# Decoding weights beside attention: one PSUM bank per unit's exponents, another order of the units, and one step earlier in a slot

## The chip, the cores and the metric

The kernel runs on one core of a Trainium2 chip. The metric is the device time of one execution in microseconds (us): 1356.4 us before the change, the median of three runs (1355.92 to 1356.41).

In the names of the profile, PE is the matrix engine (PEld its weight loads), DVE the vector engine, ACT the scalar (activation) engine, POOL the general-purpose engine, and SP the engine that issues the transfers. Each engine takes its instructions strictly in order, so an instruction that waits holds up everything behind it on its engine.

## The reference

Top-32 attention over 8 batches of 8 heads (sequence 576, head size 64), then a gated feed-forward block over the 4608 tokens:

```
scores = q @ k.T / sqrt(64)                      # per batch and head, 576 x 576
kth    = 32nd largest score of each row
attn   = softmax(where(scores >= kth, scores, -1e9))
x      = (attn @ v), heads side by side          # 4608 x 512
a, b   = x @ w1, x @ w2                          # 4608 x 1024 each
out    = ((a * b) @ w3) @ w_out                  # w3 1024 x 1024, w_out 1024 x 512
```

The weights reach the kernel as 64-bit floating-point numbers, seen as pairs of 32-bit words. Each has to be turned into 32-bit form on the chip ("decoding"). The product w3 @ w_out is formed once on the chip ("folding", tiles `pf`, `wf`), and each weight is split into a high and a low part (`wh` and `wl`, `wf[0]` and `wf[1]`) for the matmuls.

## The kernel before, in words

Attention is cut into 144 **slots**, 18 per batch; a slot is 128 query rows of two heads. Slots are pipelined over four turns p of one loop: turn p computes the scores of slot p+1 (`st`, copied to `s`), finds the 32 largest scores of slot p (DVE), masks and exponentiates slot p-1 (ACT and POOL, `pab`), and transposes slot p-2 (`tp`), multiplies it by v (`ro`) and stores it (`xt`). The feed-forward block of a batch (`ab`, `eo`) starts about two slots after the batch's last attention slot; from then on `fill` hands PE 32 of its matmuls per slot. Every engine's instructions stay in the order in which this Python code issues them.

DVE's part of a turn is a list of steps (`top32_steps`): the reciprocal of the row sums, a fold of four elementwise operations (`w`), three rounds of `MAX8` and `MATCH_REPLACE8`, a last pair of `MAX8` over 576 columns, and the store of `xt`. POOL's masking (`pab<-s,pab`) waits for the fold by an explicit dependency (lines 260 to 265).

The weights are decoded beside the first attention slots, in 80 **units** of 128x256 weights. `warm()` (line 473) is called five times in a turn, lines 497, 513, 516, 533 and 543; they are called places A to E here. Each call moves every running unit on by one step, oldest first, and starts one new unit. So units are started in the first 16 slots. A unit's steps, one for each call (lines 108 to 146):

1. ACT writes the unit's exponents `t` into PSUM and the low bits `y` into SBUF (lines 123 and 124).
2. DVE reads `t` twice, writing `z` (sign) and `y` (lines 127 and 128).
3. POOL adds the two halves of `y`.
4. Nothing.
5. For w3, PE multiplies the unit by the decoded w_out into `pf` (two matmuls; four units make one `pf`); for w1 and w2, ACT copies to `wh`. One call later come ACT's copy `wf<-pf` or POOL's `wl`, and after `wf<-pf`, another call later, DVE's `wf<-pf,wf`.

`t` and `pf` come from the same PSUM pool, `ps_m`, with three banks of 512 numbers per partition. A `t` has 256. Before, two units that follow each other share a bank (lines 106 and 114 to 117): the first takes columns 0 to 255, the second 256 to 511. The layer that sets the semaphores orders accesses by bank, so the second unit's ACT write waits until DVE has finished reading the first unit.

The units stand in a list (lines 396 to 403): 16 of w_out, then sixteen times w3, w1, w3, then 16 of w2.

Of the kernel before, what the change touches and what calls it, by code (L numbers as in the profile page):

```python
# [9 lines left out]
F32 = mybir.dt.float32  # L10
# [12 lines left out]
NCC, NFC, NEC = DM // 128, DF // 128, DM // 128  # L23
# [33 lines left out]
def attn_moe(ctx: ExitStack, tc: tile.TileContext, q, k, v, w1, w2, w3, w_out, out, flag, general):  # L57
# [23 lines left out]
    ps_m = ctx.enter_context(tc.tile_pool(name="ps_m", bufs=3, space=PSUM))  # L81
# [21 lines left out]
        sp.dma_start(z[:, :512].bitcast(I32), src)  # L103
        return z

    bank = []

    def decode(z, dst=None):

        if not bank:
            both = ps_m.tile([128, 512], F32, tag="mm", name="t")
            bank.extend((both[:, 256:], both[:, :256]))
        t = bank.pop()
        y = x_p.tile([128, 2 * HS], F32, tag="x", name="y")
        high = z[:, 1:512:2]
        low = z[:, :512].bitcast(U16)[:, 1:1024:4]  # L120
        u, r = y[:, :256].bitcast(I32), y[:, 256:512].bitcast(I32)
        sign = z[:, :256].bitcast(I32)
        act.activation(t, high, AF.Copy, scale=2.0**-112)
        act.activation(r, low, AF.Copy, scale=2.0**-13)
        yield
        ti = t.bitcast(I32)
        dve.tensor_scalar(sign, ti, -(2**31), None, op0=ALU.bitwise_and)
        dve.scalar_tensor_tensor(u, ti, 3, sign, op0=ALU.logical_shift_left, op1=ALU.bitwise_or)
        yield
        dst = y[:, :256] if dst is None else dst  # L130
        pool.tensor_tensor(dst.bitcast(I32), u, r, op=ALU.add)
        yield
        yield
        return dst

    def load_w12(i, c, z):
        if len(wl) == i:
            wl.append(const.tile([128, NCC * DF], F32R, tag="wl1", name="wl1"))
        cut = slice(c * 256, (c + 1) * 256)
        y = yield from decode(z)  # L140
        act.copy(wh[i][:, cut], y)
        yield
        pool.tensor_tensor(wl[i][:, cut], y, wh[i][:, cut].bitcast(F32), op=ALU.subtract)

    def load_wout(c, z):
        yield from decode(z, wo[:, c * 256 : (c + 1) * 256])
# [3 lines left out]
    def load_w3(c, z):  # L150
        f, i = c // 4, c % 4
        y = yield from decode(z)
        if i == 0:
            fold[f] = ps_m.tile([128, 512], F32, tag="mm", name=f"pf{f}")
        for j in range(2 * i, 2 * i + 2):
            pe.matmul(
                fold[f], y[:, (j % 2) * 128 : (j % 2 + 1) * 128], wo[:, j * DM : (j + 1) * DM],
                start=(j == 0), stop=(j == NFC - 1),
            )
        if i == 3:  # L160
            cut = slice(f * DM, (f + 1) * DM)
            yield
            act.copy(wf[0][:, cut], fold[f])
            yield
            dve.tensor_tensor(wf[1][:, cut], fold[f], wf[0][:, cut].bitcast(F32), op=ALU.subtract)
# [44 lines left out]
    def top32_steps(s, slot):  # L210

        w = att_p.tile([128, 2, S], F32, tag="w", name="w", bufs=1)
        top = tops[slot % len(tops)]
        one, two, three = slice(0, NG), slice(NG, 2 * NG), slice(2 * NG, S)
        dve.tensor_tensor(w[:, :, three], s[:, :, one], s[:, :, two], op=ALU.max)  # L220
        dve.tensor_tensor(w[:, :, two], s[:, :, one], s[:, :, two], op=ALU.min)
        dve.tensor_tensor(w[:, :, one], w[:, :, three], s[:, :, three], op=ALU.max)
        yield dve.tensor_tensor(w[:, :, three], w[:, :, three], s[:, :, three], op=ALU.min)
        for i in range(4):
            cut = slice(i * 8, (i + 1) * 8)
            for a in range(2):
                dve.max(top[:, a, cut], w[:, a, one] if i < 3 else w[:, a, :])
            if i < 3:
                for a in range(2):
                    dve.match_replace(w[:, a, one], top[:, a, cut], w[:, a, one], NEG)  # L230
                yield

    def edges_of(slot):
        top = tops[slot % len(tops)]
        edge = small.tile([128, 2, 2], F32, tag="edge", name="edge")
        pool.tensor_tensor(edge, top[:, :, 0:32:31], coef, op=ALU.mult)
        pool.tensor_tensor(over[:, 2 * slot : 2 * slot + 2], top[:, :, 31], top[:, :, 23], op=ALU.subtract)
        return edge
# [15 lines left out]
    def new_weights():  # L254
        return att_p.tile([128, 2, S], F32, tag="pab", name="pab"), small.tile([128, 2], F32, tag="sums", name="sums")
# [15 lines left out]
    def invert(sums):  # L271
        pool.tensor_scalar(sums, sums, 1e-9, None, op0=ALU.add)
        dve.reciprocal(sums, sums)
# [13 lines left out]
    def take_turned(tp, ro):  # L287
        pts = att_p.tile([128, 2, 512], F32, tag="pts", name="pts", bufs=1)
        act.copy(pts, tp)
        pr = att_p.tile([128, 128], F32, tag="pr", name="pr")  # L290
        act.copy(pr, ro[:, :128])
        return pts, pr
# [101 lines left out]
                yield  # L394

    startup = [(w_out[c], lambda z, c=c: load_wout(c, z)) for c in range(16)]
    for c in range(16):
        startup += [
            (w3[2 * c], lambda z, c=c: load_w3(2 * c, z)),
            (w1[c], lambda z, c=c: load_w12(0, c, z)),  # L400
            (w3[2 * c + 1], lambda z, c=c: load_w3(2 * c + 1, z)),
        ]
    startup += [(w2[c], lambda z, c=c: load_w12(1, c, z)) for c in range(16)]

    def new_xt():
# [52 lines left out]
    def pairs_of(i):  # L458
        return [kv[u] for u in slots[i][0]]

    def fetch_pair(u):
        if u < B * NHP:
            kv[u] = load_pair(u // NHP, u % NHP)
# [4 lines left out]
    def prefetch(n):  # L468
        while waiting and len(fetched) < n:
            src, step = waiting.pop(0)  # L470
            fetched.append((fetch(src), step))

    def warm():

        if p < 0:
            return
        if fetched:
            z, step = fetched.pop(0)
            going.append(step(z))
        going[:] = [unit for unit in going if next(unit, "end") != "end"]  # L480
        prefetch(5)
# [5 lines left out]
    for p in range(-1, n_slots + 3):  # L487
        i, j, m = p + 1, p - 1, p - 2
        if i < n_slots and slots[i][1] == 3:
            fetch_pair(slots[i][0][0] + 2)  # L490
        while starting:
            queue.append(moe_steps(*starting.pop(0), put_off.append))
        finder = top32_steps(ss[p], p) if 0 <= p < n_slots else iter(())
        if 0 <= m < n_slots:
            invert(pabs[m][1])
        folded = next(finder, None)
        warm()
        if 0 <= j < n_slots:
            edges[j] = edges_of(j)
            pabs[j] = new_weights()  # L500
            for a in range(2):
                mask(ss[j], edges[j], pabs[j][0], a, folded if a == 0 else None)
        fill(SHARE[0])
        next(finder, None)
        if 0 <= m < n_slots:
            tp, ro = turn(pabs[m][0])
            pts, pr = take_turned(tp, ro)
        if 0 <= j < n_slots:
            exps(edges[j], *pabs[j], 0)
        if ready and (m + 1) % NS:  # L510
            put_off.append(lambda x=ready[0]: split_x(x[2], x[1], 0, 1))
            starting.append(ready.pop(0))
        warm()
        fill(SHARE[1])
        next(finder, None)
        warm()
        if i < n_slots:
            st = scores(pairs_of(i), slots[i][1])
            ss[i] = new_s()
            take_scores(ss[i], st, 0)  # L520
        if 0 <= j < n_slots:
            exps(edges[j], *pabs[j], 1)
        if i < n_slots:
            take_scores(ss[i], st, 1)
        if 0 <= m < n_slots:
            us, t = slots[m]
            for u in us:
                if u not in xts:
                    xts[u] = new_xt()
            ov, rb = values([kv[u][2] for u in us], t, pts, pr, pabs[m][1], ro)  # L530
            rec = take_rb(rb)
        next(finder, None)
        warm()
        fill(SHARE[2])
        for _ in finder:
            pass
        if 0 <= m < n_slots:
            store_x([xts[u] for u in us], t, ov, rec)
            del ss[m], pabs[m], edges[m]
            if (m + 1) % NS == 0:  # L540
                ready.append((m // NS, [xts[m // NS * NHP + hp] for hp in range(NHP)], ([], [])))
                put_off.append(lambda x=ready[0]: split_x(x[2], x[1], 0, 0))
        warm()
# [63 lines left out]
```

## Time and profile before

| | |
|---|---|
| median of three runs | 1356.4 us |
| the profiled execution | 1356.2 us, of which its span is 1354.3 us |
| PE busy | 1253.2 us, 93% of the span |
| DVE busy | 1156.7 us, 85% |
| ACT busy | 981.6 us, 72% |
| POOL busy | 785.0 us, 58% |

The span is cut into 40 slices of 34 us in the page's overview. PE stands at 9 tenths or more from the ninth slice to the last but one; before that it is between 2 and 8 tenths. In those early slices DVE shows 7 to 9 tenths. The stretch in which weights are decoded is read with its own windows below, since shares over the whole span mix it with the long stretch behind it.

### The profile page before, as it was taken

Reading aid. Unit: us, or ns where it says so; the run is one execution under the profiler, and the core shown is the slowest. Engines: PE = TensorE matmul, PEld = TensorE weight load, DVE = VectorE, ACT = ScalarE, POOL = GpSimd, SP = SyncE. Lnnn points to the kernel's source line nnn. Section 1 sums busy time; section 2 is a strip of 40 time slices with the busy share of each in tenths; the row PEclk is TensorE's granted clock in tenths of the full one; section 3 lists DMA queues with packets and bytes.
Section 4 is the critical chain, followed back from the end, with each engine's and each line's share of the span. In section 5 each row is a group of like instructions: output and inputs, shape, how many; then the busy total and the mean of one; then the engine's idle time right before and its main releaser. Section 6 shows DMA issues by size and latency. Waiting matters only on the chain.

```text
span 1354.3 us, 31309 instructions
## 1 busy us (share of the span) xinstructions
PE 1253.2 (93%) x11153; PEld 1081.8 (80%) x11153; DVE 1156.7 (85%) x4060; ACT 981.6 (72%) x2169; POOL 785.0 (58%) x1033
## 2 busy tenths in 40 slices
PE   2678855899999999999999999999999999999996
PEld 1444433688989999898988898988899888989996
DVE  7998898999999999999989999999899998998100
ACT  4767777777777877787777877777777777777321
POOL 3666677665665656664656565665656565646220
PEclk6799887999999999999999999999999999999998
DMA  6443430102011111001020202010110101000000
GB/s 219 110 130 95 126 108 30 30 13 66 12 48 31 43 35 35 32 17 62 12 67 12 67 12 67 12 48 30 44 36 24 43 17 62 12 19 1 18 19 21
DMA packets 34746, 63.98 MB, mean 47 GB/s; under 512 B 3860, under 2 KB 12052, under 8 KB 34580
## 3 DMA queue, kind: packets, MB, share of 16 engines
q1 hardware_dynamic: 34580, 61.88, 14.6%
q8 instruction: 90, 1.47, 0.5%
q14 instruction: 76, 0.62, 0.1%
HBM read 52.43 MB, written 9.44 MB: 46 GB/s over the span
## 4 chain that ended last, share of the span: by engine, by line
PE 77%; DVE 13%; ACT 5%; issue 2%; POOL 2%; DMA 0%; DVEq 0%; SPq 0%; POOLq 0%; ACTq 0%
PE ab L48 29%; PE eo L48 15%; PE ro L48 14%; PE st L48 10%; PE tp L48 8%; DVE w L48 5%; DVE top L48 4%; ACT pab L48 2%; DVE y L48 2%; DVE z L48 2%; ACT pts L48 1%; ACT y L48 1%; POOL wl L48 1%; ACT t L48 1%; POOL y L48 0%
## 5 line engine op out<-in xcount | busy, mean ns | idle before, releaser
L48 POOL TENSOR_TENSOR pab<-s,pab 128x576 f32<-128x576 f32 x288 | 403.4, 1423 | 242.9 <-DVE w L48 184.7
L48 DVE MAX8 top<-w 128x8 f32<-128x192 f32 (+1 forms) x1152 | 466.7, 446 | 0.0
L48 PE MATMUL ab<-xf,wh 128*128 128x288 f32 x2048 | 432.7, 300 | 0.0
L48 PEld LDWEIGHTS ab<-xf,wh 128*128 128x128 f32 x2048 | 332.9, 188 | 8.5 <-issue 7.5
L48 PE MATMUL ab<-xf,wl 128*128 128x288 f32 x1024 | 309.5, 302 | 0.0
L48 ACT ACTIVATE pab<-s,edge 128x576 f32<-128x576 f32 x288 | 208.0, 771 | 116.2 <-POOL edge L48 115.8
L48 DVE MATCH_REPLACE8 w<-top,w 128x192 f32<-128x192 f32 x864 | 289.1, 342 | 0.0
L48 PE MATMUL st<-kt,qt 64*128 64x288 f32 (+1 forms) x1280 | 191.2, 444 | 61.0 <-ACT pts L48 51.7
L48 ACT ACTIVATE pab<-pab,edge 128x576 f32<-128x576 f32 x288 | 224.9, 781 | 20.9 <-POOL pab L48 20.5
L48 PE MATMUL eo<-g,wf 128*128 128x288 f32 x1536 | 228.2, 300 | 0.0
L48 PEld LDWEIGHTS eo<-g,wf 128*128 128x128 f32 x1536 | 208.3, 188 | 7.0 <-issue 7.0
L48 PEld LDWEIGHTS ab<-xf,wl 128*128 128x128 f32 x1024 | 192.5, 188 | 4.8 <-issue 4.8
L48 ACT COPY pts<-tp 128x1024 f32<-128x1024 f32 x144 | 145.5, 1011 | 61.8 <-PE tp L48 57.4
L48 PEld LDWEIGHTS st<-kt,qt 64*128 64x128 f32 (+1 forms) x1280 | 97.8, 181 | 115.5 <-ACT pts L48 61.6
L48 ACT COPY s<-st 128x576 f32<-128x576 f32 x288 | 181.8, 631 | 9.9 <-PE st L48 9.9
L48 POOL TENSOR_TENSOR g<-whole,g 128x288 fp32r<-128x288 f32 x128 | 103.1, 805 | 113.9 <-ACT g L48 109.9
L48 PE MATMUL tp<-ident,pab 128*128 128x128 f32 x1152 | 152.7, 275 | 16.3 <-ACT s L48 15.4
L48 DVE TENSOR_TENSOR w<-w,s 128x384 f32<-128x384 f32 x288 | 160.0, 555 | 4.9
L48 DVE TENSOR_TENSOR w<-s 128x384 f32<-128x384 f32 x288 | 155.8, 581 | 7.5 <-ACT s L48 7.5
L48 PE MATMUL ro<-pts,vt 128*64 128x128 f32 (+1 forms) x2560 | 161.1, 271 | 0.0
L48 PEld LDWEIGHTS tp<-ident,pab 128*128 128x128 f32 x1152 | 134.4, 142 | 25.5 <-POOL wo L48 13.2
L48 PEld LDWEIGHTS ro<-pts,vt 128*64 128x64 f32 x2560 | 141.3, 143 | 0.0
(49 smaller groups left out, 1275.5 us busy)
## 6 DMA issues: line engine op xcount, KB each, us to landing
z<-in_w SPq DMA_DIRECT2D x64, 256.0 KB, 2.6
vt<-in_v SPq DMA_DIRECT2D x32, 352.0 KB, 3.7
kt<-in_k SPq DMA_DIRECT2D x32, 320.0 KB, 3.5
qt<-in_q SPq DMA_DIRECT2D x32, 288.0 KB, 3.0
out_t<-osb SPq DMA_DIRECT2D x64, 144.0 KB, 1.7
z<-in_wo SPq DMA_DIRECT2D x16, 256.0 KB, 5.2
flag<-missed SPq DMA_DIRECT2D x1, 0.0 KB
seen<-flag SPq DMA_DIRECT2D x1, 0.0 KB
```

Of the source, the lines that this page charges most:

```text
L48: ins = fn(*args, **kw)
```

## The change

`decode` no longer shares a bank: each unit's `t` is a tile of its own, of which it uses half. The units of w3 and w1 stand in another order: four of w3 (one whole `pf`), then two of w1. And the call of `warm()` at place B moves ahead of the slot's first exponential (`exps(..., 0)`).

```
     def decode(z, dst=None):
-        if not bank:
-            both = ps_m.tile([128, 512], F32, tag="mm", name="t")
-            bank.extend((both[:, 256:], both[:, :256]))
-        t = bank.pop()
+        t = ps_m.tile([128, 512], F32, tag="mm", name="t")[:, :256]
...
-    for c in range(16):
-        startup += [
-            (w3[2 * c], lambda z, c=c: load_w3(2 * c, z)),
-            (w1[c], lambda z, c=c: load_w12(0, c, z)),
-            (w3[2 * c + 1], lambda z, c=c: load_w3(2 * c + 1, z)),
-        ]
+    for f in range(NFC):
+        startup += [(w3[c], lambda z, c=c: load_w3(c, z)) for c in range(4 * f, 4 * f + 4)]
+        startup += [(w1[c], lambda z, c=c: load_w12(0, c, z)) for c in range(2 * f, 2 * f + 2)]
...
             pts, pr = take_turned(tp, ro)
+        warm()
         if 0 <= j < n_slots:
             exps(edges[j], *pabs[j], 0)
         if ready and (m + 1) % NS:
             put_off.append(lambda x=ready[0]: split_x(x[2], x[1], 0, 1))
             starting.append(ready.pop(0))
-        warm()
         fill(SHARE[1])
```

What this does to ACT's order shows in the eighth slot, the one whose fold starts at 93.95 us in the trace of before. In before, ACT has there, from the last unit of the slot before (place E) to the unit of place B (`t_907` is one bank, used twice; `pab,sums` is the exponential):

```order
L48 ACTIVATE t_907<-z_770 128x256
...
L48 ACTIVATE t_907<-z_787 128x256
L48 ACTIVATE y_931<-z_787 128x256
L48 ACTIVATE pab_939<-s_725,edge_936 128x576 x2
L48 COPY pts_960<-tp_949 128x1024
L48 COPY pr_962<-ro_958 128x128
L48 ACTIVATE pab_939,sums_940<-pab_939,edge_936 128x576
L48 CAST wh0_98<-y_841 128x256
L48 ACTIVATE t_969<-z_827 128x256
L48 ACTIVATE y_970<-z_827 128x256
```

In the changed kernel the same stretch of ACT's order reads (every `t` has a number of its own):

```order
L48 ACTIVATE t_924<-z_785 128x256
...
L48 ACTIVATE t_948<-z_803 128x256
L48 ACTIVATE y_949<-z_803 128x256
L48 ACTIVATE pab_957<-s_740,edge_954 128x576 x2
L48 COPY pts_978<-tp_967 128x1024
L48 COPY pr_980<-ro_976 128x128
L48 CAST wf0_100<-pf2_851 128x512
L48 CAST wh0_98<-y_858 128x256
L48 ACTIVATE t_987<-z_843 128x256
L48 ACTIVATE y_988<-z_843 128x256
L48 ACTIVATE pab_957,sums_958<-pab_957,edge_954 128x576
```

The unit of place B, with the copies of older units, now stands ahead of the exponential instead of behind it. Through the pool, from the first `pf` to the last every `pf` gets the same bank, and the `t` of successive units alternate between the other two: `t_987` waits for DVE to have read the unit two before it, `t_924`.

On PE, in the same slot, the fold's matmuls stood in before as follows, from the transposes to the end of the values:

```order
L48 MATMUL tp_949<-ident_85,pab_792 128x128 x8
L48 MATMUL ro_958<-ident_85,pab_792 128x128
L48 MATMUL pf2_834<-wo_102,y_892 128x512 x2
L48 MATMUL st_990<-kt_122,qt_120 128x288 x2
...
L48 MATMUL pf3_1019<-wo_102,y_908 128x512 x2
L48 MATMUL pf3_1019<-wo_102,y_970 128x512 x2
```

And in the changed kernel:

```order
L48 MATMUL pf2_851<-wo_102,y_840 128x512 x2
L48 MATMUL tp_967<-ident_85,pab_808 128x128 x8
L48 MATMUL ro_976<-ident_85,pab_808 128x128
L48 MATMUL st_1010<-kt_122,qt_120 128x288 x2
...
L48 MATMUL pf3_1039<-wo_102,y_925 128x512 x2
L48 MATMUL pf3_1039<-wo_102,y_949 128x512 x2
L48 MATMUL pf3_1039<-wo_102,y_988 128x512 x2
```

A `pf` is now filled by units that follow each other, and some calls of `warm()` issue no matmul. The next `pf` starts in the call after DVE's `wf<-pf,wf` of the one before, whose bank it takes over.

## Rows read from the trace of the kernel before

**Rows 1.** The page, busy time, share of the span and instructions of each engine.

```profile
PE 1253.2 (93%) x11153; PEld 1081.8 (80%) x11153; DVE 1156.7 (85%) x4060; ACT 981.6 (72%) x2169; POOL 785.0 (58%) x1033
```

**Rows 2.** Windows: four stretches, and what the columns are.

```profile
core 0: us, PE busy (x) PEld busy (x) DVE busy (x) ACT busy (x) POOL busy (x), PEclk, DMA share, GB/s
20.00:206.00 186.00, 128.33 (x714) 71.60 (x714) 167.92 (x520) 133.59 (x326) 123.50 (x163) 0.84 0.40 116
206.00:256.00 50.00, 31.39 (x267) 22.30 (x268) 45.09 (x159) 38.79 (x86) 35.31 (x47) 0.82 0.09 28
256.00:300.00 44.00, 43.80 (x422) 38.79 (x420) 41.42 (x149) 33.69 (x72) 27.07 (x35) 1.00 0.08 24
300.00:1250.00 950.00, 950.00 (x9009) 853.69 (x9010) 881.10 (x3177) 742.55 (x1608) 571.16 (x747) 1.00 0.11 35
```

**Rows 3.** Waits, 20 to 206: who waited for whom, us, times, longest.

```profile
ACT t L48 <- DVE y L48: 53.1, 34, 4.3
...
DVE z L48 <- ACT y L48: 9.2, 7, 1.8
...
DVE wf L48 <- ACT wf L48: 2.5, 2, 1.2
```

**Rows 4.** Waits of DVE, 206 to 290.

```profile
DVE sums L48 <- POOL sums L48: 3.3, 4, 1.1
DVE z L48 <- ACT y L48: 2.0, 2, 1.8
```

**Rows 5.** Timeline, slot from 93.95: start, us, instruction [idle before, releaser].

```profile
93.54 0.42 DVE L48 SCALAR_TENSOR_TENSOR y<-t,z 128x256 int32<-128x256 int32 x1
...
93.95 1.53 DVE L48 TENSOR_TENSOR w<-s 128x384 f32<-128x384 f32 x2
94.11 0.96 POOL L48 TENSOR_TENSOR y<-y 128x256 int32<-128x256 int32 x1 [0.32 <-DVE sums L48]
...
95.41 1.14 DVE L48 TENSOR_TENSOR w<-w,s 128x384 f32<-128x384 f32 x2
...
96.92 0.42 DVE L48 SCALAR_TENSOR_TENSOR y<-t,z 128x256 int32<-128x256 int32 x1
...
97.38 0.40 ACT L48 ACTIVATE t<-z 128x256 f32<-128x256 f32 x1 [4.07 <-DVE y L48]
...
98.04 1.42 ACT L48 ACTIVATE pab<-s,edge 128x576 f32<-128x576 f32 x2
...
98.87 2.77 POOL L48 TENSOR_TENSOR pab<-s,pab 128x576 f32<-128x576 f32 x2 [2.86 <-DVE z L48]
...
100.42 0.78 ACT L48 ACTIVATE pab<-pab,edge 128x576 f32<-128x576 f32 x1
...
101.48 0.40 ACT L48 ACTIVATE t<-z 128x256 f32<-128x256 f32 x1
...
101.82 0.44 ACT L48 ACTIVATE y<-z 128x256 int32<-128x256 uint16 x1
...
102.28 0.42 DVE L48 TENSOR_SCALAR z<-t 128x256 int32<-128x256 int32 x1 [1.80 <-ACT y L48]
...
106.70 0.68 DVE L48 TENSOR_TENSOR wf<-pf,wf 128x512 fp32r<-128x512 f32 x1
```

**Rows 6.** Timeline, the next slot, to the fold of the one behind it.

```profile
108.24 1.54 DVE L48 TENSOR_TENSOR w<-s 128x384 f32<-128x384 f32 x2
...
112.43 0.78 ACT L48 ACTIVATE pab<-pab,edge 128x576 f32<-128x576 f32 x1
...
116.64 0.64 ACT L48 COPY s<-st 128x576 f32<-128x576 f32 x1
...
120.03 1.54 DVE L48 TENSOR_TENSOR w<-s 128x384 f32<-128x384 f32 x2
```

**Rows 7.** Groups by form, DVE, first 20 to 206, then 300 to 1250.

```profile
L48 DVE TENSOR_TENSOR w<-s 128x384 f32<-128x384 f32 x28 | 22.4, 840 | 0.0
...
L48 DVE TENSOR_TENSOR w<-s 128x384 f32<-128x384 f32 x234 | 118.5, 547 | 0.0
```

More of the change, by code (lines that the diff above doesn't have):

```diff
@@ L104, in fetch @@
         return z
-    bank = []
     def decode(z, dst=None):
-        if not bank:
-            both = ps_m.tile([128, 512], F32, tag="mm", name="t")
-            bank.extend((both[:, 256:], both[:, :256]))
-        t = bank.pop()
+        t = ps_m.tile([128, 512], F32, tag="mm", name="t")[:, :256]
         y = x_p.tile([128, 2 * HS], F32, tag="x", name="y")
```

## The prediction

> **What bounds the kernel now.** I read the page's shares first, then windows by stage, then the waits of the stage that the change touches, then a timeline of two slots in it. The page says PE 93% [rows 1], which would make a change to weight decoding look irrelevant; the windows say otherwise. From 300 to 1250 us PE is busy for all 950.00 us, and from 256 to 300 for 43.80 of 44: there PE is the bound, and nothing in it changes. From 20 to 206, where the weights are decoded, PE has work for 128.33 of 186 us and DVE for 167.92 [rows 2]. That stage is DVE's.
>
> The feed-forward matmuls of a batch become available only when its 18 slots are through, so PE cannot use the idle time of the early stage for later work. From 256 on PE does not stop. So what is cut from the early slots moves the whole rest forward by the same amount: one microsecond of early slot is one microsecond of the end. The question is how much of DVE's early time is waiting.
>
> DVE is idle for 186 - 167.92 = 18.1 us there. The waits name 9.2 (7 times) on ACT's `y` of a decoded unit and 2.5 (2 times) on ACT's copy `wf` [rows 3]; after 206 there are 2.0 more (2 times) on `y` [rows 4]. The other 18.1 - 9.2 - 2.5 = 6.4 us up to 206 lie between 520 instructions and in small waits; I take them to stay.
>
> What the waits come from shows in the slot that begins at 93.95 [rows 5]. ACT stood still for 4.07 us before `t` at 97.38, released by DVE's `y` of 96.92, which ends at 97.34. That DVE instruction is the decode of the unit before, in the other half of the same bank, and DVE comes to it only after its fold. Behind this `t` on ACT stand the masks of the slot (98.04), so POOL's masking starts at 98.87 after 2.86 us idle, although the fold it must wait for ended at 95.41 + 1.14 = 96.55. So the exponential starts at 100.42, and the `t` of place B behind it at 101.48, its `y` at 101.82. DVE wanted them 1.80 us before it got them, at 102.28. The next slot has no such stall: its exponential starts 112.43 - 108.24 = 4.2 us after the fold, against 100.42 - 93.95 = 6.5. It is 120.03 - 108.24 = 11.79 us long against 14.29 [rows 5, 6]. The difference of 2.50 is the stall of 1.80 and the `wf<-pf,wf` of 0.68 that only the first has. With five units in a slot and two to a bank, the stall comes in every other slot.
>
> **The change part by part.**
>
> *A bank for each unit.* ACT's `t` of a unit no longer waits for the unit just before it. In all ACT waited 53.1 us in 34 such waits [rows 3]; most of it costs nothing, because ACT is not the bound. What counts is what reached DVE. With two banks left for `t` (the third holds `pf`), a `t` waits for the decode two units back. In the slot at 93.95 that is the DVE instruction at 93.54, done at 93.96 [rows 5], so the masks no longer wait for the fold plus a decode. Masking can then start when the fold is done, 96.55 instead of 98.87: 2.3 us earlier, more than the 1.80 of the stall.
>
> *Place B ahead of the exponential.* It takes ACT's `t` and `y` for place B out of the exponential's shadow: they need only the decode two units back, done at 97.34. Price: exponential, second exponential and the copies of the scores come later by `t` and `y`, 101.82 + 0.44 - 101.48 = 0.78 us, and in some slots by a copy `wf` or `wh` as well. Cover: in the undisturbed slot the last `s<-st` ends at 116.64 + 0.64 = 117.28 and the next fold, which needs it, starts at 120.03 [rows 6], so 2.7 us are free. Were this cover gone, it would be 0.78 x 16 slots = 12.5 us. Below nothing the move can bring no more than the 13.7 us summed below, which the banks alone may bring already. I take 0 beside the banks, as 0.78 is well under 2.7.
>
> *The order of the units.* Same 80 units, same instructions. With four of w3 together a `pf` lives for a stretch that ends before the next begins, which leaves it one bank. The next `pf` starts one call behind DVE's `wf<-pf,wf`, so PE waits for DVE where it did not; queued behind it are the scores in a few slots (where it falls at place C). The scores have the same 2.7 us. DVE's `wf<-pf,wf` stays 8 times 0.68. Two units of w1 in a row put two `wl` of POOL close together; POOL was busy for 123.50 of 186 us [rows 2] and has room. I take 0, with 2.5 us as the upper bound (all waits on `wf` staying as they are) and the same again below.
>
> *The transfers.* One step of place B moves past one exponential on ACT alone; on SP and POOL it passes nothing. The units are fetched five ahead, with the same sizes, and no wait on a transfer stands in the stalls.
>
> *POOL beside the fold.* The two `w<-s` of a fold took 840 ns each in this stage against 547 later [rows 7]; at 93.95 a weight addition of POOL (0.96) lies on them [rows 5]. That is 28 x 0.293 = 8.2 us in the stage. The Trainium skill says (SBUF — State Buffer, "Who interferes with whom") that a DVE instruction with two SBUF inputs contends with a POOL instruction that reads SBUF; the trace agrees, 840 against 547. By that rule a denser early stage could put more of POOL's additions on folds, which speaks against the change. POOL's addition is released by DVE's decode just ahead of the fold, before and after, so I take 0. Bounds: all of it gone, -8.2; all of the 28 + 28 operations of the folds hit as hard as one is hit per fold now (0.59), 56 x 0.59 - 8.2 = +24.8.
>
> *Sum.* 9.2 + 2.5 + 2.0 = 13.7 us of DVE's waits go. Against the profiled execution: 1356.2 (span 1354.3 and 1.9 around it) - 13.7 = 1342.5. That execution lies 0.2 below the median of the runs, so 1342.7 is the forecast for the median.
>
> **What is late next.** In the slots without the stall DVE is late itself: 11.79 us of almost unbroken work. So the waits removed should not uncover another engine; ACT, busy for 133.59 of 186 us, is next, with room.
>
> **The rivals.**
>
> *Half of it comes back as a wait for banks.* The Trainium skill notes (Perfetto Trace Analysis, "Identifying Performance Opportunities") that the same gap repeating on an engine can mean that there is not enough PSUM. A bank for each unit halves the number of units that fit. As a mechanism here: `t` of place B waits for the decode behind the fold (97.34), and copies `wf` and `wh` of 0.6 and 0.4 stand ahead of it, so in the slots that have them its `y` ends near 97.34 or the end of `pr` plus 1.0 + 0.78, about 100, when DVE asks for it at 102.28 - 1.80 = 100.48. That is short cover. For it: only 0.5 us. Against: the copies are in few slots. Half of 13.7 staying gives 1349.5.
>
> *The stalls only move.* If the exponentials, now later on ACT, make DVE wait for `sums` (1.1 us at worst after 206, [rows 4]) or the scores, 12 waits of 1.1 would eat 13.2: 1356, no change. Against it: sums and scores have 2.7 us of cover. It is also the case in which the change does not do what it says.
>
> *Slower: POOL on the folds.* With the stalls gone, POOL's additions and `wl` fall on more of the folds' operations. Each costs 0.59. It decides the sign from 13.7 / 0.59 = 23 more operations of the 56; all of them would give 1342.7 + 24.8 = 1367.5. For it: 840 against 547 ns. Against it: what POOL runs beside a fold is released by the same DVE instruction as before.
>
> *Faster still:* the additions leave the folds, 1342.7 - 8.2 = 1334.5. For it: POOL's masking starts earlier, so its queue is emptier when the next fold begins.
>
> **How the numbers follow.** Forecast 0.68; half back 0.14; faster still 0.08; stalls only moved 0.05; slower 0.05. The forecast's own range is 1339 to 1346: 2.5 us for the fold waits either way, and about 1 for the rest. For 8 in 10 it has to reach toward half back and toward faster still: 1337 to 1350. That leaves out the ends, about 0.18. Under 0.2% (2.7 us) a measurement of this kernel can't be told from no change. Faster: 0.68 + 0.14 + 0.08 = 0.90; same 0.05; slower 0.05.
>
> **What would show it.** In the profile after: ACT's waits of `t` for DVE's `y` far below 53.1 us and none of 4 us; DVE's waits for ACT's `y` and `wf` nearly gone; folds 11.5 to 12.6 us apart in every slot and no longer by turns; POOL's masking directly behind the fold; the window from 300 on still with PE busy throughout, and PE's first unbroken stretch beginning about 13.7 us earlier than 256. Wrong would be: DVE waits of over 1 us in the decoding stage under another name (`sums`, `s`), `w<-s` at another mean than 840 ns, or slots of 13 us and more.

## The result, and the profile after

The changed kernel takes 1342.65 us (median of four runs, 1342.13 to 1344.63) against 1356.33 for the kernel before, four runs beside it: a ratio of 0.9902, with a 95% interval from 0.9885 to 0.992. That is 13.7 us less. The profiled execution took 1342.86 us, its span 1340.9.

The page of the changed kernel, which answers to [rows 1], shows that no engine has less to do:

```profile
PE 1253.7 (93%) x11153; PEld 1082.8 (81%) x11153; DVE 1156.0 (86%) x4060; ACT 980.9 (73%) x2169; POOL 785.2 (59%) x1033
```

The windows of the changed kernel, each about 13 to 14 us earlier than its partner in [rows 2], with the same columns:

```profile
20.00:193.00 173.00, 125.60 (x714) 70.81 (x714) 166.14 (x514) 132.37 (x324) 123.92 (x163) 0.88 0.42 125
193.00:242.00 49.00, 34.45 (x267) 24.05 (x267) 46.16 (x165) 37.86 (x85) 34.81 (x46) 0.74 0.10 29
242.00:286.00 44.00, 43.78 (x418) 38.78 (x418) 41.22 (x149) 33.70 (x72) 26.76 (x35) 1.00 0.08 24
286.00:1236.00 950.00, 950.00 (x9009) 853.55 (x9008) 881.28 (x3177) 742.05 (x1607) 571.77 (x747) 1.00 0.11 35
```

Behind the decoding nothing has changed: PE is busy for 43.78 of 44 us from 242 on, as it was for 43.80 of 44 from 256 on, and for all 950 us of the next stretch, with the same 9009 matmuls in it. All of the gain lies before. There DVE was idle for 18.1 of 186 us and is now idle for 173 - 166.14 = 6.9 of 173; in the stretch behind it, the second row, its idle time went from 4.9 to 2.8 us. Together that is 13.3 us.

The waits of the changed kernel from 20 to 193, which answer to [rows 3]:

```profile
PE pf L48 <- DVE wf L48: 18.5, 7, 3.9
...
ACT t L48 <- DVE y L48: 9.0, 10, 2.0
...
DVE z L48 <- ACT y L48: 0.7, 2, 0.4
```

ACT's waits for DVE fell from 53.1 to 9.0 us, DVE's waits for ACT's `y` from 9.2 to 0.7, and those for `wf` are gone. In their place PE waits 18.5 us for DVE's `wf<-pf,wf`: every `pf` now takes over the bank of the one before.

The timeline of the changed kernel, in the same slot as [rows 5], to the next fold:

```profile
90.54 1.54 DVE L48 TENSOR_TENSOR w<-s 128x384 f32<-128x384 f32 x2
90.59 0.41 ACT L48 ACTIVATE t<-z 128x256 f32<-128x256 f32 x1 [0.96 <-DVE y L48]
...
90.70 0.97 POOL L48 TENSOR_TENSOR y<-y 128x256 int32<-128x256 int32 x1 [1.40 <-DVE sums L48]
...
92.17 1.44 ACT L48 ACTIVATE pab<-s,edge 128x576 f32<-128x576 f32 x2 [0.81 <-POOL edge L48]
...
93.31 2.78 POOL L48 TENSOR_TENSOR pab<-s,pab 128x576 f32<-128x576 f32 x2 [0.71 <-DVE w L48]
...
96.11 0.44 ACT L48 ACTIVATE t<-z 128x256 f32<-128x256 f32 x1
...
96.46 0.45 ACT L48 ACTIVATE y<-z 128x256 int32<-128x256 uint16 x1
...
96.80 0.77 ACT L48 ACTIVATE pab<-pab,edge 128x576 f32<-128x576 f32 x1
...
97.07 0.68 DVE L48 TENSOR_TENSOR wf<-pf,wf 128x512 fp32r<-128x512 f32 x1
...
97.66 0.41 DVE L48 TENSOR_SCALAR z<-t 128x256 int32<-128x256 int32 x1
...
103.01 1.54 DVE L48 TENSOR_TENSOR w<-s 128x384 f32<-128x384 f32 x2
```

The first `t` starts 0.05 us after the fold does, not 3.43 after it, and the masks (92.17) wait for their own input, `edge`, and no longer for a `t`. POOL's masking starts 2.77 us after the start of the fold; in [rows 5] it was 4.92. Place B's `y` is done at 96.91, and DVE comes to it at 97.66 without waiting. The slot is 12.47 us long, against 14.29.

### The profile page after: what moved, and what is told of

Same layout as the page of the kernel before. It is cut to its first block, busy times and chain, and to the rows that moved or that the text cites. A ratio compares the mean times of both kernels' runs of the same rounds, so it can differ in the third digit from the quotient of the medians.

```text
span 1340.9 us, 31351 instructions
## 1 busy us (share of the span) xinstructions
PE 1253.7 (93%) x11153; PEld 1082.8 (81%) x11153; DVE 1156.0 (86%) x4060; ACT 980.9 (73%) x2169; POOL 785.2 (59%) x1033
## 4 chain that ended last, share of the span: by engine, by line
PE 79%; DVE 14%; POOL 2%; issue 2%; ACT 2%; DMA 0%; DVEq 0%; SPq 0%; POOLq 0%; ACTq 0%
PE ab L48 29%; PE eo L48 16%; PE ro L48 14%; PE st L48 11%; PE tp L48 8%; DVE w L48 6%; DVE top L48 4%; DVE y L48 2%; DVE z L48 2%; PE pf L48 1%; ACT pab L48 1%; POOL y L48 1%; POOL wl L48 1%; ACT pts L48 0%; POOL pab L48 0%
```

## The experiments

Three explanations were held against each other. **Masks**: what costs is a `t` at place A that waits for the decode of the unit just before, because the slot's masks stand behind it on ACT. **Exponential**: what costs is that place B stands behind the exponential. **Banks**: every wait on a shared bank costs, wherever it stands. All runs were timed beside the kernel before, whose medians were 1355.98 to 1356.44 us.

**Parts of the change.** `banks_order` leaves out the move of place B; `move_only` is nothing but this move; `banks_only` is nothing but the first hunk of the change, `order_only` nothing but the new list of units.

> The change without its third part: own banks and the new order of units, but place B stays behind the slot's first exponential. Theory 'masks' (the stall comes from the unit at place A, whose exponents wait for the decode just before them and hold up the slot's masks behind them on ACT): nearly all of the gain stays, 1343 to 1345 us, DVE's waits for y and wf under 2 us in the decoding stage. Rival 'exponential' (the gain comes from place B standing ahead of the exponential): most of the gain is gone, 1352 to 1356. Rival 'banks' (every wait on a shared bank costs, wherever it stands): 1343 as well.

> Only the third part: banks shared by two units and the old order of units, but place B ahead of the first exponential. 'Masks': the masks are still late in every other slot, but place B's unit no longer waits behind the exponential; it can run when pr is copied (100.52 in the slot shown) plus 0.4 for a copy in some slots, so y ends at 101.3 to 101.7 and DVE's stall shrinks from 1.8 to about 0.8 to 1.2; 9 stalls less 0.8 each: 1348 to 1351. 'Exponential': the whole gain, 1343. 'Banks': no gain, 1356.

> Own banks alone; old order of units, place B behind the exponential. With the old order two pf live at once for a while, which leaves one bank to the exponents, so waits on the unit just before come back, but only one of them at place A (unit 50), and one unit at place A (unit 45) waits for DVE's wf just behind the fold. 'Masks': two stalls of 1.5 to 2 us remain, 1345 to 1348. If the order of the units carried a good part of the gain: over 1350.

> The new order of units alone: shared banks, place B behind the exponential. Units of odd number at place A still wait for the unit just before, in every other slot. 'Masks': no gain, 1355 to 1358. If the order of the units carried a good part: under 1352.

| | us | ratio to before, 95% interval |
|---|---|---|
| banks_order | 1344.4 | 0.9914, 0.9897 to 0.993 |
| move_only | 1349.58 | 0.995, 0.9933 to 0.9966 |
| banks_only | 1342.15 | 0.9896, 0.9879 to 0.9912 |
| order_only | 1355.56 | 0.9995, 0.9986 to 1.0005 |

The banks alone carry the whole gain, and most of it is there without the move (`banks_order`), where "exponential" expected 1352 to 1356. The move alone brings half of the gain, as expected: DVE's nine waits of [rows 3] fall from 11.7 to 6.0 us, but ACT still waits as before, 49.1 us from 20 to 205 in both. DVE's and ACT's waits in `move_only`, 20 to 205:

```profile
DVE z L48 <- ACT y L48: 5.0, 7, 1.0
DVE wf L48 <- ACT wf L48: 1.0, 2, 0.5
```

```profile
ACT t L48 <- DVE y L48: 49.1, 28, 4.2
```

With the banks there, neither of the other two parts adds anything that these runs can tell. For `banks_only` 1345 to 1348 was expected, for two stalls that should remain. Less remains (three waits of DVE for `y`, 1.2 us at most, 2.2 in all). PE's wait for `wf`, which the new order brings, is not among the waits of `banks_only`; that its absence makes up for the stalls left was not tested.

**The same sharing, placed otherwise.** Both kernels have the new order and place B behind the exponential. `pairs_in_slot` shares banks, two units to one, but begins anew in each slot: A with B, C with D, E alone. `pairs_on_a` gives each unit its own bank, but for place A, which shares with the unit just before it.

```
-        t = ps_m.tile([128, 512], F32, tag="mm", name="t")[:, :256]
+        k = count[0]
+        count[0] += 1
+        if k % 5 in (1, 3):          # pairs_on_a: if k and k % 5 == 0
+            t = bank.pop()
+        else:
+            both = ps_m.tile([128, 512], F32, tag="mm", name="t")
+            bank[:] = [both[:, 256:]]
+            t = both[:, :256]
```

> Banks are still shared, but by the units of places A and B and of C and D, with E alone: the unit at place A then never waits for the unit just before it. New order of units; place B behind the exponential as before. Two waits on the unit just before in each slot, 32 in all, about as many as in before. 'Masks': the gain is there, 1343 to 1346. 'Exponential': 1356. 'Banks': 1354 to 1356.

> The opposite: only the unit at place A shares a bank with the unit just before it (place E of the slot before), in each of the 15 slots from the second on; all others have their own. New order; place B behind the exponential. 15 waits on the unit just before in place of 40. 'Masks': every slot has the stall that every other slot of before has, 15 times about 1.5 us over the changed kernel, 1362 to 1368, slower than before. 'Exponential': 1356. 'Banks': 15/40 of the loss, 1347 to 1349.

`pairs_in_slot` took 1342.73 us (0.9901, 0.9885 to 0.9918), `pairs_on_a` 1364.62 (1.0063, 1.0046 to 1.008). So 32 shared units, not far from the 40 of before, cost nothing when none stands at place A, and 15 make the kernel slower than before when all of them do. ACT's waits in `pairs_in_slot`, 20 to 205, and then DVE's and ACT's in `pairs_on_a`, same stretch:

```profile
ACT t L48 <- DVE y L48: 14.7, 24, 1.3
```

```profile
DVE z L48 <- ACT y L48: 17.7, 14, 1.8
DVE wf L48 <- ACT wf L48: 2.5, 2, 1.3
```

```profile
ACT t L48 <- DVE y L48: 60.0, 14, 6.6
```

Fourteen waits at place A are longer in sum than the 34 of [rows 3], and now every slot has its stall. In these two kernels place and length go together: the waits at place A are 1.9 to 6.6 us long, since DVE comes to that decode only behind its fold, and none of ACT's in `pairs_in_slot` is over 1.3. That it is what stands behind the wait that counts is shown by `move_only`, where ACT waits as long as before and half of the loss is gone, and by `clear_shared` below. Two slots of `pairs_on_a` that follow each other, DVE alone:

```profile
98.33 1.53 DVE L48 TENSOR_TENSOR w<-s 128x384 f32<-128x384 f32 x2
...
112.48 1.54 DVE L48 TENSOR_TENSOR w<-s 128x384 f32<-128x384 f32 x2
...
120.54 0.42 DVE L48 TENSOR_SCALAR z<-t 128x256 int32<-128x256 int32 x1 [1.46 <-ACT y L48]
...
126.42 1.54 DVE L48 TENSOR_TENSOR w<-s 128x384 f32<-128x384 f32 x2
```

They are 14.15 and 13.94 us long; the two slots of before in [rows 5, 6] are 14.29 and 11.79. "Exponential" falls with `pairs_in_slot` too, "banks" with both.

**What POOL's additions cost the fold.** In the changed kernel the two `w<-s` still take 850 ns on average. Two kernels take POOL's addition away from the fold. `a_behind_masks` calls place A, with all steps of the units there, behind the masks:

```
         folded = next(finder, None)
-        warm()
...
             for a in range(2):
                 mask(ss[j], edges[j], pabs[j][0], a, folded if a == 0 else None)
+        warm()
```

`pool_late` instead moves the addition to the fourth step of a unit.

> The changed kernel with the call at place A moved behind the slot's masks, so that POOL's weight addition is queued behind the masking and no longer runs beside DVE's fold. If POOL's addition is what makes the first two operations of the fold take 840 to 850 ns on average against 547 later, they fall to about 550 and 8 us go: 1334 to 1337. If the lengthening has another cause (or the addition only hits another operation): 1341 to 1344. PE's fold matmul at place C then waits for an addition behind the masking, which may delay scores and cost up to 1 us in some slots.

> The changed kernel with POOL's addition one call later in each unit (third step empty, fourth step the addition). At place A POOL then adds a unit that DVE finished well before the end of the slot before, so the addition can be over when the fold starts, without waiting behind the masking. Same two theories as for a_behind_masks: 1334 to 1338 if the addition lengthens the fold, 1341 to 1344 if not.

Both were slower than the changed kernel: 1347.5 us (0.9933, 0.9917 to 0.995; this interval just touches that of the changed kernel) and 1361.74 (1.0046, 1.0029 to 1.0063), and the expectation missed. The fold itself did what was expected in `a_behind_masks`, and in part in `pool_late`. The group in the changed kernel (20 to 193), in `a_behind_masks` (20 to 206) and in `pool_late` (20 to 205):

```profile
L48 DVE TENSOR_TENSOR w<-s 128x384 f32<-128x384 f32 x28 | 22.7, 850 | 0.0
```

```profile
L48 DVE TENSOR_TENSOR w<-s 128x384 f32<-128x384 f32 x28 | 14.2, 546 | 0.0
```

```profile
L48 DVE TENSOR_TENSOR w<-s 128x384 f32<-128x384 f32 x26 | 15.3, 629 | 0.0
```

The 8.5 us gained in `a_behind_masks` came back elsewhere, and more. DVE's waits in `a_behind_masks`, 20 to 205, and in its slot that begins at 114.97 the timeline of how they come about:

```profile
DVE xt L48 <- ACT rec L48: 8.5, 7, 2.1
DVE z L48 <- ACT y L48: 3.4, 11, 0.4
```

```profile
116.45 1.88 PE L48 MATMUL pf<-wo,y 128*128 128x512 f32 x4
117.21 2.77 POOL L48 TENSOR_TENSOR pab<-s,pab 128x576 f32<-128x576 f32 x2 [2.78 <-DVE w L48]
119.94 2.77 POOL L48 TENSOR_TENSOR y<-y 128x256 int32<-128x256 int32 x4
120.71 3.29 PE L48 MATMUL pf<-wo,y 128*128 128x512 f32 x4 [2.38 <-POOL y L48]
123.93 1.58 PE L48 MATMUL st<-kt,qt 64*128 64x288 f32 x8
125.08 0.64 ACT L48 COPY s<-st 128x576 f32<-128x576 f32 x1 [4.50 <-PE st L48]
...
127.02 0.27 ACT L48 COPY rec<-ro 128x128 f32<-128x128 f32 x1
127.32 0.29 DVE L48 TENSOR_TENSOR xt<-ro,rec 128x128 f32<-128x128 f32 x1 [2.13 <-ACT rec L48]
```

POOL's additions now stand behind the masking. PE's fold matmul needs one of them and stands ahead of the scores on PE, so the scores, their copies and `rec` are late, and DVE waits for `rec`. In `pool_late` the addition comes one call later and PE asks for it in the next; there the same wait is longer. PE's and DVE's waits in `pool_late`, 20 to 205:

```profile
PE pf L48 <- POOL y L48: 25.7, 9, 5.5
```

```profile
DVE xt L48 <- ACT rec L48: 17.6, 7, 4.6
```

**Taking this wait away.** `clear_fold` is `a_behind_masks` with one empty step more ahead of the matmuls of a w3 unit, so that PE asks for an addition one call later. `clear_fold_c` in addition calls place C behind the scores and their first copy.

```
     def load_w3(c, z):
         f, i = c // 4, c % 4
         y = yield from decode(z)
+        yield
...
-        warm()                                  # clear_fold_c
         if i < n_slots:
             st = scores(pairs_of(i), slots[i][1])
             ss[i] = new_s()
             take_scores(ss[i], st, 0)
+        warm()                                  # clear_fold_c
```

> The changed kernel with the call at place A behind the slot's masks, and each w3 unit's matmuls one call later. In a_behind_masks the fold ran at 546 ns but PE's fold matmul at place C stood ahead of the scores and waited for an addition that was now behind the masking; scores, ro and rec came late and DVE waited up to 2.1 us for rec. If that is what took the gain back, it comes back here: folds at 546 ns and waits for rec under 2 us in total, 1333 to 1337. If DVE waits for rec for another reason (POOL or ACT behind by a whole call), 1342 to 1348.

> clear_fold with the call at place C behind the scores and their first copy, so that neither the fold's matmuls nor ACT's copies of wh at place C stand ahead of the scores. If scores are still late for these in clear_fold, 1 to 3 us less than clear_fold, down to 1332; if not, the same within 1 us, or up to 2 us more because place C's unit comes later to DVE.

They took 1336.8 us (0.9857, 0.9839 to 0.9876) and 1335.15 (0.985, 0.9833 to 0.9866), and the gain of the fold is there. The fold and DVE's wait for `rec` in `clear_fold`, 20 to 200:

```profile
L48 DVE TENSOR_TENSOR w<-s 128x384 f32<-128x384 f32 x30 | 15.2, 546 | 0.0
```

```profile
DVE xt L48 <- ACT rec L48: 2.3, 3, 1.4
```

Whether place C adds anything is not decided: the intervals of the two overlap.

Two last kernels start from `clear_fold_c`. `clear_old_order` has the old list of units again. `clear_shared` has no part of the change under study at all: it is the kernel before, with place A behind the masks, the empty step, and place C behind the first copy of the scores.

> clear_fold_c with the old order of units (w3, w1, w3). In the new order each pf takes over the bank of the one before, and PE waits for DVE's wf (10.7 us in clear_fold_c between 60 and 200), after which its granted clock is low. In the old order two pf live at once, PE does not wait for wf, and the waits of the exponents on the unit just before that come back at place A no longer hold up the masks, which now stand ahead of place A. 'Masks': as fast or up to 3 us faster than clear_fold_c, 1332 to 1335.5. If a wait on the unit just before costs wherever it stands: 1338 or more.

> The kernel before, with no part of the change: shared banks, old order, place B behind the exponential; only place A behind the masks, each w3 unit's matmuls one call later, and place C behind the first copy of the scores. About 40 waits on the unit just before remain, but none stands ahead of the masks. 'Masks': the stalls go and the folds run at about 546 ns, 1334 to 1340. 'Banks': the stalls of before stay and only the 8 us of the folds go, 1346 to 1350.

`clear_old_order` took 1332.95 us (0.9828, 0.9811 to 0.9844), the fastest kernel here, and `clear_shared` 1335.56 (0.9847, 0.9831 to 0.9863). ACT's and DVE's waits in `clear_shared`, 20 to 190:

```profile
ACT t L48 <- DVE y L48: 27.7, 27, 2.2
```

```profile
DVE z L48 <- ACT y L48: 1.5, 4, 0.5
```

ACT still waits 27 times, but with the masks ahead of place A DVE waits only 1.5 us for `y`. The stalls can be removed without a bank for each unit, by standing the masks ahead of the waiting instruction: that is "masks" shown from the other side. The longest of these waits is 2.2 us; one of 4 us behind the masks was not tried. `clear_old_order` is `clear_shared` with the banks and the move of place B, and 2.6 us faster: the runs of the two do not overlap (1332.62 to 1333.37 and 1335.25 to 1335.83), the intervals of the ratios do. Against `clear_fold_c`, `clear_old_order` has a median 2.2 us lower; the intervals overlap. In its profile PE's wait for `wf` is not among the waits, as expected.

## Why the prediction was right, step by step

The forecast was 1342.7 us, the measurement 1342.65. That it came so near is partly luck: the interval of the ratio alone is worth 2.3 us to either side.

- *The stage is DVE's, and what it saves moves the rest as a block.* Right: the windows behind the decoding are the same, 14 us earlier, and the span is 13.4 us shorter.
- *A bank for each unit: the masks no longer wait for fold and decode; 13.7 us of DVE's waits go.* Right in mechanism (`pairs_on_a`, `pairs_in_slot`, `clear_shared`) and in size: 13.0 of the 13.7 went, 0.7 for `y` stayed. The rest of DVE's idle time was taken to stay at 6.4 us, and stayed at 6.9 - 0.7 = 6.2. That 2.3 us of earlier masking suffice for a stall of 1.80 is shown by `banks_order` and `banks_only`, which have the gain without the move.
- *Place B ahead of the exponential: 0 beside the banks, and no more than they bring already.* Right as far as the runs can tell. By itself the move is worth 6.5 us, by shortening the stall, which the prediction did not work out.
- *The order of the units: 0, PE waiting for `wf`.* Right within the runs; the wait is there (18.5 us). With a bank for each unit the old order has the lower median in both pairs of kernels that differ in the order alone, by 2.2 us (`banks_only` against `banks_order`, `clear_old_order` against `clear_fold_c`); neither is clear of the noise, and both are within the bound of 2.5 us. One sign of being wrong came up: slots of 13 us and more. The intervals from fold to fold that begin at 64.32 and 140.12 are 13.69 and 13.06 us, against 11.5 to 12.6 forecast. In these two PE waits longest for `wf`, and the eight `pf` matmuls behind the wait take over 5 us (granted clock 0.69 and 0.70), where eight take 3.70 at 76.07 in the same trace (PE, changed kernel):

```profile
68.22 5.30 PE L48 MATMUL pf<-wo,y 128*128 128x512 f32 x8 [3.85 <-DVE wf L48]
...
143.47 5.22 PE L48 MATMUL pf<-wo,y 128*128 128x512 f32 x8 [3.74 <-DVE wf L48]
```

The scores stand behind these matmuls. They still came in time, with their last copy done 1.8 us ahead of the next fold, where the prediction counted on 2.7. What stands behind that copy on ACT did not: DVE waited 0.36 us for `y` in both slots and 0.21 for `rec` in the first. It was idle for 0.98 and 0.90 us in these slots, against 0.34 to 0.49 in the others from 78.01 to 178.10. A third such wait, 3.14 us at 112.39, stands behind the scores of its slot; that slot is 12.39 us long.

- *POOL beside the fold: 0.* Right: 840 before, 850 after. The reason given is nearly so: the profile names not DVE's decode as what releases the addition but mostly `sums`, the reciprocal between that decode and the fold, before and after ([rows 5]; 90.70 in the changed kernel). The price read from the rows, 8.2 us, is about what `a_behind_masks` freed (8.5). The Trainium skill's rule (SBUF — State Buffer, "Who interferes with whom"), that a DVE instruction with two SBUF inputs contends with a POOL instruction that reads SBUF, is borne out by 850 against 546 ns. POOL's addition is longer as well: 0.97 us at 90.70, beside the fold, and 0.73 at 97.42, behind it.
- *Stalls only moved; slower by POOL on the folds.* Neither came. A trace of the second is in the slot at 64.32, where a `wl` of POOL and an addition lie on the fold together: its second pair of operations took 1.69 us, and 1.14 in the slot at 90.54.
- *Half back as a wait for banks.* Did not come. The short cover was seen rightly: 0.5 us was worked out, 97.66 - 96.91 = 0.75 measured in that slot.
- *Faster still.* Its ground, an earlier masking that leaves POOL's queue emptier, was wrong: at 90.70 POOL had stood idle for 1.40 us, against 0.32 in [rows 5], and the addition still came with the fold, since DVE releases it. It had to be moved.

## What to carry to other kernels

When one engine waits in order for another, ask what stands behind the waiting instruction, and not only how long it waits: 14 waits ahead of the masks cost more than the 34 of before, and 27 with the masks ahead of place A let 1.5 us through to DVE. The cure is then either to remove the wait or to issue the urgent work ahead of it, and the second needs no memory. When an instruction is moved behind other work on one engine, look at once at who consumes its result and what stands behind that consumer: the fold's 8.5 us came back as a wait for `rec`, three engines further on.

## What was not expected of the hardware

A short wait of PE can cost more than its own length. In the slot of `a_behind_masks` shown above PE stood still for 2.38 us. The windows before, in and after it; the granted clock is the number before the last two:

```profile
117.00:118.30 1.30, 1.30 (x4) 0.27 (x2) 1.27 (x6) 1.16 (x4) 1.09 (x1) 1.00 0.01 3
118.30:120.70 2.40, 0.03 (x1) 0.00 (x0) 2.37 (x13) 1.95 (x5) 2.40 (x4) 1.00 0.38 109
120.70:124.00 3.30, 3.29 (x6) 1.03 (x6) 3.09 (x12) 0.00 (x0) 2.01 (x3) 0.58 0.58 156
```

The granted clock was 1.00 (2.4 GHz) before the wait and 0.58 over the stretch behind it, in which it stood at the lower level (0.50, 1.2 GHz) from 121.5 to 124. Four `pf` matmuls took 3.29 us where four just before had taken 1.88. The 1.4 us more stood ahead of the scores. It does not always come so: in the same kernel PE stood still for 3.14 us ahead of four `pf` matmuls at 136.44 and for 2.91 us ahead of eight at 111.96, and these took 1.98 and 3.67 us, at a granted clock of 1.00:

```profile
136.44 1.98 PE L48 MATMUL pf<-wo,y 128*128 128x512 f32 x4 [3.14 <-POOL y L48]
```

So the length of the wait alone does not decide it; what does is not shown.

The executions of the changed kernel lie further apart (1342.13 to 1344.63 us) than those of before (1355.92 to 1356.41). That is not because the stalls are gone: in `banks_only`, `pairs_in_slot`, `clear_old_order` and `clear_shared`, where they are gone too or nearly so, the executions of a kernel lie within 1.2 us. In all six kernels with both a bank for each unit and the new order they lie 2.4 to 4.8 us apart, and in no other kernel here over 1.4. Why was not tested.
